# Loading the operands of an attention backward pass in nine pieces per pair of heads instead of seventeen

## The chip, the cores and the metric

The kernel runs on one core of a Trainium2 chip. A core has five engines with instruction streams of their own: TensorE (PE in the profile, PEld for its weight loads), VectorE (DVE), ScalarE (ACT), GpSimd (POOL) and SyncE (SP). They wait for one another through semaphores, and 16 DMA engines, shared by all queues, move data between HBM and the on-chip memory (SBUF). The metric is the device time of one execution in microseconds (us), lower is better; each time given is the median of several runs.

## What is computed

The reference is a transformer block (layer norm with modulation, softmax attention with 32 heads of 16 features over 2048 tokens and a width of 512, then a squared-ReLU MLP), its output, and the gradients of nine of its inputs. The change touches only the backward pass of the attention:

```python
scores = jnp.einsum('bhqd,bhkd->bhqk', q, k) * scale
p = _softmax(scores, axis=-1)
o = jnp.einsum('bhqk,bhkd->bhqd', p, v)
...
_out, _vjp = jax.vjp(_f, A_x, A_wqkv, A_wo, B_w1, B_b1, B_w2, B_b2, c, w_mod)
_grads = _vjp(grad_out)
```

For each head the backward pass forms the probabilities again (P = exp of Q K^T), the products dP = dO V^T, dS = P * dP, and from these the gradients dV = P^T dO, dK = dS^T Q and dQ = dS K.

## The kernel before

The program first runs the forward pass with much of the MLP in its shadow (`phase_fwd`, `phase5`'s setup), then `attn_bwd`, then the weight gradients and the input gradient (`phase6`). In `attn_bwd` the 32 heads are 8 groups of four (`g`), each handled as two pairs (`jp`). One such **pass** over a pair has 64 **steps**, one for each chunk `c` of 512 keys and each block `ib` of 128 queries. Four steps with the same `dsg` tile are called a **stretch** here (`m` from 0 to 15). The order of the instructions on each engine is as written: the scheduler is off in this phase.

A step does, for both heads `a` of the pair:

- PE computes the scores (`st`, line 1608), 64 rows of `QT` against `masked["KT"][a]`, in which only the rows of head `a` are not zero. ACT takes their exponential into `pu` (line 1611).
- PE computes dP of the step before (`dp`, line 1522), 64 rows of `dOT` against `masked["VT"][a]`. DVE multiplies it with `pu` into `ds` (line 1526); in some stretches, for one block, ACT copies it out and POOL multiplies instead (lines 1540 and 1541).
- PE accumulates dK and dV (`kv`, line 1459) some steps later, with the token-major `Q` and `dO` as weights.
- After four steps SP issues one DMA transpose of the 128 x 4096 tile `ds` into one of five buffers (`dsT`, line 1549; the fifth is part of `keep`). In one stretch of four PE transposes an eighth of it. Two such transposes feed eight `dq` calls (line 1484, weights from the token-major `K`); these are made in the even steps of the eight that follow the issue of the next two transposes' second one. So PE first needs a transposed tile about two stretches after the later of its two transposes was issued.

The operands lie in HBM in two forms. By features: `QTq_d`, `KTq_d`, `VTq_d`, `dOTq_d`, 128 rows for the four heads of a group, 32 rows for each, of 2048 tokens; a head uses rows 0 to 15 of its 32 for Q and K, and rows 0 to 17 for V and dO (two rows more, which carry the softmax's row term), and the other rows are zero. By tokens: `ktm_d` (128 x 2048 for a group), `qtm_d` and `dOp_d` (128 x 1024 each).

While group g is worked on, group g+1 is loaded into the other of two sets of tiles (names with a final g, and `q` or `keep` for the other set; the first two groups' loads fill whole tiles, all later ones only the rows that change). The list of these **pieces** is made by `load_group`; `pair_pieces` gives the four pieces of K^T and V^T for the next pair, and one or two pieces of a weight for the next phase (`wmt`) go between. The loop at lines 1594 to 1597 spreads a pass's pieces evenly over its 16 stretches. All are issued by POOL, in its instruction order, and before each stands a one-element copy from the `ds` tile of the stretch before (`tick`, line 1596), which holds POOL until DVE has begun that tile, so that the loads keep pace with the work. POOL's own multiplications (line 1541) stand in the same queue.

Of the kernel before, what the change touches and what calls it, by code (L numbers as in the profile page):

```python
# [19 lines left out]
P = 128  # L20
DH = 16
# [4 lines left out]
def chunks(total, size):  # L26
    out = []
    s = 0
    while s < total:
        w = min(size, total - s)  # L30
        out.append((s, w))
        s += w
    return out
# [72 lines left out]
class K:  # L106
# [1284 lines left out]
    def load_group(self, g):  # L1391

        S, ST, qp = self.S, self.ST, self.qp
        tm = {"K": self.ktm_d, "Q": self.qtm_d, "dO": self.dOp_d}
        fm = {"QT": (self.QTq_d, DH), "dOT": (self.dOTq_d, DH + 2)}
        width = {n: S if n in fm else ST * P if n == "K" else ST * 4 * DH for n in (*fm, *tm)}
        if g < 2:
            T, o = {}, 0
            for n, e in width.items():
                if g:  # L1400
                    T[n] = qp.tile([P, e], BF16, name=f"{n}g")[:]
                elif n == "K":
                    T[n] = self.keep[:, :e]
                else:
                    T[n] = self.q0[:, o:o + e]
                    o += e
            self.Tq[g] = T
        T, pieces = self.Tq[g % 2], []
        for n, (src, rows) in fm.items():
            if g < 2:  # L1410
                pieces += [(T[n][:, s0:s0 + sw], src[g, :, s0:s0 + sw]) for (s0, sw) in chunks(S, 1024)]
            else:
                pieces += [(T[n][r:r + rows, :], src[g, r:r + rows, :]) for r in range(0, P, 32)]
        for n, src in tm.items():
            pieces += [(T[n][:, a:a + 256], src[g, :, a:a + 256]) for a in range(0, width[n], 256)]
        return {n: t if n in fm else t.rearrange("p (st w) -> p st w", st=ST) for n, t in T.items()}, pieces

    def wq_pieces(self, t):
# [3 lines left out]

    def pair_pieces(self, g, jp):
        pieces = []
        for n, src, sh, rows in (("KT", self.KTq_d, 0, DH), ("VT", self.VTq_d, 2, DH + 2)):
            for j in (2 * jp, 2 * jp + 1):
                r = 32 * ((j + sh) % 4)
                pieces.append((self.masked[n][j % 2][r:r + rows, :], src[g, r:r + rows, :]))
        return pieces
# [536 lines left out]
```

## Time and profile before

| | |
|---|---|
| runs | 2509.63, 2515.87, 2516.81 us; median 2515.87 |
| profiled execution, first to last instruction (span) | 2498.5 us |
| median less this span | 17.4 us |
| attention backward | from 1166.9 us to about 2376.5 us of the span |
| busy in the whole span | PE 96%, ACT 91%, DVE 68%, POOL 30% |
| the 16 DMA engines | 90% busy or more in nearly every slice of the backward phase |

The profile does not give the profiled execution's time outside its span; if it was like the median of the runs, 17.4 us lie around the span. A page of the profile has, among others, the chain of work that ended last, the waits (which engine waited at which line for which other), groups of instructions with their mean duration, and the DMA queues: q1 is the hardware queue that carries SP's transposes, q0 the software queue that POOL issues to. For a line of DMA instructions, SPq and POOLq are the issuing sequencers, and "to landing" is the time from issue until the data is there.

### The profile page before, as it was taken

How to read it: one execution, taken by the hardware profiler on the slowest of the kernel's cores; microseconds unless marked ns; L12 is line 12 of the kernel's file. 1: busy time of each engine (PE TensorE's matmuls, PEld its weight loads, DVE VectorE, ACT ScalarE, POOL GpSimd, SP SyncE). 2: the span in 40 equal slices, each digit the busy share in tenths (PEclk: the TensorE clock that was granted, in tenths of full speed). 3: DMA queues.
4: the chain of work that ended last, by engine and by line, in shares of the span. 5: the costliest groups of instructions: out<-in, count | busy, mean ns of one | idle time of the engine just before them, and what ended most of it. 6: DMA issues, size and time to landing. Idle time of an engine off the chain costs nothing.

```text
span 2498.5 us, 67897 instructions
## 1 busy us (share of the span) xinstructions
PE 2410.2 (96%) x26211; PEld 1061.6 (42%) x26439; DVE 1695.0 (68%) x3487; ACT 2283.1 (91%) x3757; POOL 753.5 (30%) x1337
## 2 busy tenths in 40 slices
PE   8999999999999999999999999999999999999998
PEld 4555555555555555583233332333333333333343
DVE  6222322422332343576999999999999999999957
ACT  7999999999999997534999999999999999999945
POOL 2344531220131022245222323322333222322223
PEclk9999999999999999999999999999999999999999
DMA  4589661541243045499999999999999999999997
GB/s 166 135 179 208 169 125 47 132 100 40 92 114 98 23 123 147 110 199 216 232 235 233 232 227 231 237 234 231 230 235 239 234 230 236 234 233 236 238 217 192
DMA packets 1293547, 454.13 MB, mean 182 GB/s; under 512 B 1236948, under 2 KB 1261398, under 8 KB 1293222
## 3 DMA queue, kind: packets, MB, share of 16 engines
q1 hardware_dynamic: 1252422, 344.68, 71.8%
q0 software_dynamic: 38720, 104.04, 13.9%
q8 instruction: 207, 3.39, 0.6%
q10 hardware_dynamic: 2080, 1.05, 0.2%
q14 instruction: 118, 0.97, 0.1%
HBM read 75.83 MB, written 64.49 MB: 56 GB/s over the span
## 4 chain that ended last, share of the span: by engine, by line
PE 49%; ACT 35%; DMA 7%; issue 5%; DVE 3%; POOL 1%; SPq 1%; ACTq 0%; DVEq 0%; POOLq 0%
ACT pu L391 26%; PE st L1608 17%; PE acckv L1459 8%; ACT pu L1611 6%; DMA dsT<-ds 5%; PE accq L1484 5%; PE st L388 4%; PE dp L1522 2%; PE accbank L322 2%; PE dps L1050 2%; PE dp L1659 1%; PE st L1754 1%; ACT csq L1540 1%; PE pps L1237 1%; DVE ds L1526 1%
## 5 line engine op out<-in xcount | busy, mean ns | idle before, releaser
L1526 DVE TENSOR_TENSOR ds<-dp,pu 128x512 bf16<-128x512 f32 x1888 | 1166.0, 682 | 34.6 <-PE dp L1522 19.1
L1611 ACT ACTIVATE pu<-st 128x512 bf16<-128x512 f32 x2048 | 1073.8, 666 | 34.7 <-PE st L1608 21.3
L391 ACT ACTIVATE pu<-st 128x1024 bf16<-128x1024 f32 x992 | 912.1, 1077 | 4.2 <-PE st L388 3.7
L388 PE MATMUL st<-QTm,KTq 128*128 128x512 bf16 x1859 | 560.9, 377 | 27.1 <-ACT pu L391 6.1
L322 PEld LDWEIGHTS <-pu 128*128 128x128 bf16 x8192 | 346.7, 96 | 236.1 <-issue 3.0
L1522 PE MATMUL dp<-kvm,q 64*128 64x512 bf16 x1024 | 365.0, 384 | 2.0 <-DVE ds L1526 0.7
L322 PE MATMUL accbank<-Vaug,pu 128*128 128x17 bf16 x8192 | 357.4, 171 | 8.3 <-ACT Vaug L522 1.1
L1522 PE MATMUL dp<-kvm,dOTg 64*128 64x512 bf16 x1024 | 363.6, 383 | 0.3
L1608 PE MATMUL st<-kvm,q 64*128 64x512 bf16 x1024 | 349.4, 382 | 5.4 <-ACT pu L1611 0.2
L1608 PE MATMUL st<-kvm,QTg 64*128 64x512 bf16 x1024 | 348.1, 381 | 6.5
L1541 POOL TENSOR_TENSOR ds<-csq,pu 128x512 bf16<-128x512 f32 x128 | 147.2, 1150 | 627.0 <-ACT csq L1540 553.6
L388 PEld LDWEIGHTS <-KTq 128*128 128x128 bf16 x1984 | 188.4, 96 | 176.9 <-issue 124.8
L1459 PE MATMUL acckv<-ds,Qg 128*16 128x512 bf16 x1024 | 176.2, 382 | 0.3
L1459 PE MATMUL acckv<-pu,q 128*16 128x512 bf16 x1024 | 176.3, 383 | 0.0
L1459 PE MATMUL acckv<-ds,q 128*16 128x512 bf16 x1024 | 176.2, 383 | 0.0
L1459 PE MATMUL acckv<-pu,dOg 128*16 128x512 bf16 x1024 | 176.0, 382 | 0.0
L302 POOL DMA_DIRECT2D QTm<-QTq_d x124 | 63.1, 511 | 341.5 <-PE st L388 320.0
L1608 PEld LDWEIGHTS <-q 64*128 64x128 bf16 x1024 | 67.0, 94 | 163.5 <-issue 150.6
L1608 PEld LDWEIGHTS <-QTg 64*128 64x128 bf16 x1024 | 67.1, 94 | 160.6 <-issue 145.7
L329 DVE RECIPROCAL rl<-accbank 128x4 f32<-128x4 f32 x128 | 22.9, 179 | 158.3 <-PE accbank L322 158.2
L1522 PEld LDWEIGHTS <-q 64*128 64x128 bf16 x1024 | 88.8, 93 | 52.9 <-issue 43.3
L1522 PEld LDWEIGHTS <-dOTg 64*128 64x128 bf16 x1024 | 88.2, 93 | 52.9 <-issue 43.8
(390 smaller groups left out, 3055.1 us busy)
## 6 DMA issues: line engine op xcount, KB each, us to landing
KTq<-KTq_d POOLq DMA_DIRECT2D x24, 512.0 KB, 3.9
duT_d<-auT POOLq DMA_DIRECT2D x3, 1792.0 KB, 7.9
aT_d<-rT POOLq DMA_DIRECT2D x3, 1792.0 KB, 11.5
KTq_d<-KTq SPq DMA_DIRECT2D x32, 128.0 KB, 2.1
QTq_d<-ev_fm SPq DMA_DIRECT2D x32, 128.0 KB, 4.3
ktm_d<-ev_tm POOLq DMA_DIRECT2D x32, 128.0 KB, 2.5
VTq_d<-vT POOLq DMA_DIRECT2D x4, 1024.0 KB, 6.3
dx<-dx_d SPq DMA_DIRECT2D x16, 256.0 KB, 4.6
```

What stands on the lines that cost most here:

```text
L302: nc.gpsimd.dma_start(QTm[j][32 * j:32 * j + 32, :], self.QTq_d[g, 32 * j:32 * j + 32, 512 * qc:512 * (qc + 1)])
L322: nc.tensor.matmul(acc[:, a, sub, :], lhsT=pu[:, a, sub * P:(sub + 1) * P], rhs=Vaug[:, kb, h, :], start=(kb == 0 and a == 0 and sub == 0) ...
L388: nc.tensor.matmul(stt[:, a, :], lhsT=KT[:, kb * P:(kb + 1) * P], rhs=QTm[2 * jp + a][:], start=True, stop=True)
L391: nc.scalar.activation(pu[:], stt[:], ACT.Exp, scale=self.scale)
L1050: nc.tensor.matmul(pt[:], lhsT=a[st], rhs=g_tm[:, st, :], start=(st == 0), stop=(st == ST - 1))
L1459: nc.tensor.matmul(acckv[r:r + DH, :], lhsT=T[n][:, ib, col:col + DH], rhs=src[:, a, :], start=(ib == 0), stop=(ib == ST - 1))
L1484: nc.tensor.matmul(accq[r:r + 32, o:o + 256], lhsT=T["K"][:, 4 * c + sub, col:col + 32], rhs=v[:, r // 32 % 2 * 2:r // 32 % 2 * 2 + 2, 4 * ...
L1522: nc.tensor.matmul(dp[:], lhsT=T["dOT"][rd, ib * P:(ib + 1) * P], rhs=masked["VT"][a][rd, 512 * c:512 * (c + 1)], start=True, stop=True)
L1526: nc.vector.tensor_tensor(dsg[:, i, a], dp[:], pu[:, a, :], ALU.mult)
L1541: nc.gpsimd.tensor_tensor(dsg[:, i, 1], f[:], pu[:, 1, :], ALU.mult)
L1608: nc.tensor.matmul(stt[:], lhsT=T["QT"][rs, q], rhs=masked["KT"][a][rs, c0:c0 + 512], start=True, stop=True)
L1611: nc.scalar.activation(pu[:, a, :], stt[:], ACT.Exp, scale=self.scale)
```

## The change

For groups 2 to 7, Q^T comes in two pieces of 48 rows (two heads and the 16 rows between them) instead of four of 16, and dO^T in two of 64 rows instead of four of 18. By tokens, K, Q and dO come in pieces of 1024 columns instead of 256, for group 1 too: two, one and one instead of eight, four and four. V^T of each head comes as 32 rows instead of 18. The extra rows hold zeros or are multiplied by zeros, so the results are the same. The loads of group 0 stay as they were except for V^T's rows, and so do the weights' pieces and those of the last two passes.

```diff
         tm = {"K": self.ktm_d, "Q": self.qtm_d, "dO": self.dOp_d}
-        fm = {"QT": (self.QTq_d, DH), "dOT": (self.dOTq_d, DH + 2)}
+        fm = {"QT": (self.QTq_d, 32 + DH), "dOT": (self.dOTq_d, 64)}
...
-                pieces += [(T[n][r:r + rows, :], src[g, r:r + rows, :]) for r in range(0, P, 32)]
+                pieces += [(T[n][r:r + rows, :], src[g, r:r + rows, :]) for r in range(0, P, 64)]
         for n, src in tm.items():
-            pieces += [(T[n][:, a:a + 256], src[g, :, a:a + 256]) for a in range(0, width[n], 256)]
+            pieces += [(T[n][:, a:a + w], src[g, :, a:a + w]) for a, w in chunks(width[n], 1024 if g else 256)]
...
-        for n, src, sh, rows in (("KT", self.KTq_d, 0, DH), ("VT", self.VTq_d, 2, DH + 2)):
+        for n, src, sh, rows in (("KT", self.KTq_d, 0, DH), ("VT", self.VTq_d, 2, 32)):
```

Since a pass's pieces are spread evenly over its 16 stretches, fewer pieces also stand in other stretches. With 17 pieces there is about one in each; with nine they fall in stretches 0, 2, 4, 6, 8, 9, 11, 13 and 15. POOL has 1067 instructions in its list instead of 1283: 108 loads and 108 ticks fewer. The lists of PE, ACT and DVE are the same but for buffer numbers.

The first place is POOL's list in the first pass (group 0, first pair), where Q^T and dO^T of group 1 are loaded in four pieces of 128 rows x 1024 columns. `ds<-csq` and `ds<-junk_19880` are POOL's multiplications, `kvm` holds K^T and V^T, `QTg` and `dOTg` are the tiles of group 1. Before:

```order
 L1597 DMA WmT<-WmT_d 128x384
 L1541 TENSOR_TENSOR ds<-csq,pu 128x512
 L1596 COPY tick<-ds 1x1
 L1597 DMA QTg<-QTq_d 128x1024
 L1596 COPY tick<-ds 1x1
 L1597 DMA QTg<-QTq_d 128x1024
 L1541 TENSOR_TENSOR ds<-csq,pu 128x512
 L1596 COPY tick<-ds 1x1
 L1597 DMA dOTg<-dOTq_d 128x1024
 L1596 COPY tick<-ds 1x1
 L1597 DMA dOTg<-dOTq_d 128x1024
```

and now:

```order
 L1597 DMA WmT<-WmT_d 128x384
 L1596 COPY tick<-ds 1x1
 L1597 DMA QTg<-QTq_d 128x1024
 L1541 TENSOR_TENSOR ds<-csq,pu 128x512
 L1541 TENSOR_TENSOR ds<-junk_19880,pu 128x512
 L1596 COPY tick<-ds 1x1
 L1597 DMA QTg<-QTq_d 128x1024
 L1541 TENSOR_TENSOR ds<-csq,pu 128x512
 L1596 COPY tick<-ds 1x1
 L1597 DMA dOTg<-dOTq_d 128x1024
 L1541 TENSOR_TENSOR ds<-csq,pu 128x512
 L1541 TENSOR_TENSOR ds<-junk_19880,pu 128x512
```

The four loads stood in two couples, with one multiplication of POOL between the couples; now one or two multiplications stand between any two of them.

The second place is the end of a second pass and the start of the next, for the token-major Q and dO of group 2 (tile `q_19184`). Before, four loads of Q and four of dO of 256 columns stood there, of which this is the end:

```order
 L1597 DMA q_19184<-qtm_d 128x256
 L1596 COPY tick<-ds 1x1
 L1597 DMA q_19184<-dOp_d 128x256
 L1541 TENSOR_TENSOR ds<-csq,pu 128x512
 L1596 COPY tick<-ds 1x1
 L1597 DMA q_19184<-dOp_d 128x256
 L1541 TENSOR_TENSOR ds<-junk_19880,pu 128x512
 L1596 COPY tick<-ds 1x1
 L1597 DMA q_19184<-dOp_d 128x256
```

and now the two loads are:

```order
 L1597 DMA q_19184<-qtm_d 128x1024
 L1541 TENSOR_TENSOR ds<-csq,pu 128x512
 L1541 TENSOR_TENSOR ds<-junk_19880,pu 128x512
 L1596 COPY tick<-ds 1x1
 L1597 DMA q_19184<-dOp_d 128x1024
 L1541 TENSOR_TENSOR ds<-csq,pu 128x512
 L1596 COPY tick<-ds 1x1
 L1597 DMA kvm<-KTq_d 16x2048
```

The whole of dO now comes as the last load of the pass, behind POOL's two multiplications of stretches 13 and 14 and before the one of stretch 15.

## The prediction

> **What bounds the kernel now.** I first cut the backward phase into its 16 passes, at the first exponential of each, and read the busy times by window: the length of a pass, busy time and count of PE, of its weight loads, of DVE, ACT and POOL, the clock, the DMA share (over 1 where packets overlap) and GB/s.
>
> ```profile
> core 0: us, PE busy (x) PEld busy (x) DVE busy (x) ACT busy (x) POOL busy (x), PEclk, DMA share, GB/s
> 1166.90:1245.30 78.40, 72.92 (x704) 20.78 (x703) 73.06 (x119) 73.54 (x145) 22.30 (x40) 0.98 1.06 211
> 1245.30:1319.90 74.60, 73.91 (x805) 23.30 (x804) 73.36 (x119) 74.38 (x153) 21.48 (x41) 1.00 1.19 233
> ...
> 1470.30:1547.80 77.50, 74.82 (x805) 22.88 (x804) 73.61 (x119) 75.31 (x154) 22.60 (x45) 1.00 1.26 223
> ...
> 2148.90:2223.50 74.60, 73.92 (x805) 23.30 (x804) 73.34 (x119) 74.38 (x153) 22.78 (x45) 1.00 1.22 238
> 2223.50:2298.80 75.30, 74.36 (x805) 23.15 (x804) 73.57 (x119) 74.63 (x153) 18.08 (x31) 1.00 1.21 231
> 2298.80:2376.50 77.70, 75.03 (x817) 25.67 (x816) 74.04 (x121) 76.27 (x155) 22.29 (x43) 1.00 1.18 235
> sum 1209.60, PE 1187.48 PEld 371.20 DVE 1174.87 ACT 1194.52 POOL 356.14; mean PE 74.22 PEld 23.20 DVE 73.43 ACT 74.66 POOL 22.26
> ```
>
> A pass without a stall takes 74.6 us, and in it PE, ACT and DVE are all busy over 73 us. That is a floor which no load moves. What loads can move is the rest. The 14 passes from 1245.3 to 2298.8 take 1053.5 us, which is 14 x 74.6 = 1044.4 and 9.1 us more. The first pass has 78.4 - 74.6 = 3.8 us more, the last 3.1.
>
> The waits of the backward phase (from 1166 to 2390 us; total, times, longest) name what the rest is made of:
>
> ```profile
> POOL ds L1541 <- ACT csq L1540: 553.6, 115, 8.1
> ACT pu L1611 <- PE dp L1522: 9.3, 19, 2.8
> PE accq L1484 <- DMA dsT<-ds: 7.4, 12, 2.9
> PEld L1608 <- DMA keep<-ktm_d: 0.5, 2, 0.2
> ```
>
> POOL waits for the others and nobody waits long for it, so its instructions are free here. PE almost never waits for a loaded operand (0.5 us in two waits). It waits for late transposes, 12 times, and behind the waiting `accq` matmul stand the next scores and dP, so ACT and DVE lose the same time a little later. The instructions of line 1549 and their landing say how near the edge this is (ns min/median/max, then us):
>
> ```profile
> L1549 SPq DMA_TRANSPOSE dsT<-ds x208: 3490/4262/6457, 1173.4 to 2377.8; - x104
> ...
> DMA to landing us min/median/max: 5.1/7.2/9.0
> ```
>
> SP has one transpose to issue each 74.6/16 = 4.66 us, and issuing takes a median of 4.26. So SP and the DMA engines behind it have about 0.4 us to spare in each, some 6 us in a pass. A tile is wanted about two stretches, 9.3 us, after its issue was due.
>
> **What a load costs the transposes.** Of two passes, the quiet one from 2148.9 and the last from 2298.8, the DMA queue's packets, MB and share of 16 engines, and the last one's loads:
>
> ```profile
> q0 software_dynamic: 592, 1.16, 4.5%
> ...
> q0 software_dynamic: 768, 2.10, 7.8%
> ...
> keep<-xhat_d POOLq DMA_DIRECT2D x16, 128.0 KB, 4.1
> ```
>
> The quiet pass spends 4.5% of 74.6 us, 3.4 us of all 16 engines, on 1.16 MB: 2.9 us for 1 MB, 0.19 us for a piece of 64 KB and 0.76 for one of 256 KB. The bad case is in the first pass, where four pieces of 256 KB stand in two couples. POOL's rows, the queue from 1195 to 1215 us, the chain, and the wait in that pass:
>
> ```profile
> 1195.98 0.59 POOL L1597 DMA_DIRECT2D QTg<-QTq_d  x1
> ...
> 1197.78 0.54 POOL L1597 DMA_DIRECT2D QTg<-QTq_d  x1 [0.26 <-issue]
> ...
> 1204.86 0.58 POOL L1597 DMA_DIRECT2D dOTg<-dOTq_d  x1
> ...
> 1207.00 0.54 POOL L1597 DMA_DIRECT2D dOTg<-dOTq_d  x1 [0.26 <-issue]
> ...
> q0 software_dynamic: 304, 1.01, 20.9%
> ...
> 1206.13 11.04 DMA dsT<-ds
> ...
> PE accq L1484 <- DMA dsT<-ds: 2.9, 1, 2.9
> ```
>
> 20.9% of 20 us is 4.2 us for 1.01 MB, so 1.1 us for each 256 KB. A transpose issued among them landed after 11.04 us, PE waited 2.9 us for it, and the pass was 3.8 us over the floor. 11.04 - 2.9 = 8.1: a landing of up to about 8 us costs nothing, which is 0.9 us above the median.
>
> **The change, part by part.**
>
> *Fewer instructions on POOL.* 108 loads and 108 ticks go. Line 1597 by tile (ns min/median/max) and the tick's group in two passes from 1817 us (count, busy us, mean ns, idle before) give the price:
>
> ```profile
> L1597 POOL DMA_DIRECT2D Kg<-ktm_d x32: 534/565/580, 1214.5 to 2186.9; - x32
> L1597 POOL DMA_DIRECT2D kvm<-VTq_d x30: 498/544/568, 1179.2 to 2245.3; - x30
> ...
> L1596 POOL COPY tick<-ds 1x1 bf16<-1x1 bf16 x34 | 6.0, 176 | 13.8 <-DVE ds L1526 13.8
> ```
>
> About 0.56 + 0.18 us each, 80 us in all, whatever a load's size, but of an engine that is busy 22 us of a pass and issues for 17 x 0.56 = 9.5 more, out of 75. Worth nothing in time; if POOL were the bound it would be worth the 80.
>
> *More bytes.* A group's loads were 2304 KB: 256 for K^T, 288 for V^T, 192 of weights, 256 for Q^T, 288 for dO^T, 512, 256 and 256 by tokens. Now V^T and dO^T are 512 each and Q^T is 384, in all 2880 KB, a quarter more. At 2.9 us for 1 MB the 0.29 MB more of a pass take 0.85 us of DMA time, at the first pass's price 1.2. Either fits in the 6 us to spare, so in the sum it costs 0; without that room it would cost 14 x 0.85 = 12 us.
>
> *The first pass.* Its couples are taken apart: as the rows of order show, one or two of POOL's multiplications stand between any two of the four loads, which fall in stretches 9, 11, 13 and 15, about 9 us apart. One piece then costs a transpose about 1 us, from a median of 7.2 to 8.2 us, at the edge. I take back 3 of the 3.8 us; the ends are 3.8 and 0.
>
> *The other 14 passes.* In the first half of a pass there is now one piece of 64 to 128 KB in two stretches where there were two of 64 to 72, so what is late there gets a little better. In the second half four pieces of 192 to 256 KB stand about 9 us apart, each instead of two of 64 to 72. A transpose that meets one is later by 0.76 to 1.1 us, where before it met two at 0.2 each: 0.4 to 0.7 us worse. The waits start at about 8 us, above the median of 7.2, so a part of the transposes crosses it. I put the gain and the loss at about 3 us each and take 0. The ends are -9.1 us (every stall gone) and +53 (each pass stalls as the first did, 14 x 3.8).
>
> *Operands that land later as one piece.* The whole of dO now comes last, in stretch 15, while dK and dV of the next group first want it in that group's fourth step. In POOL's order it stands right behind the multiplication of stretch 14, so it is issued a stretch and more before the pass ends, 8 us before its use. The rows of 256 KB before:
>
> ```profile
> QTg<-QTq_d POOLq DMA_DIRECT2D x2, 256.0 KB, 5.1
> dOTg<-dOTq_d POOLq DMA_DIRECT2D x2, 256.0 KB, 7.6
> ```
>
> 5.1 to 7.6 us, the latter in the bunch; that hides it. Landing 1 us beyond would cost 1 us in each of 6 changes of group.
>
> Sum: 0 + 0 - 3 + 0 + 0 = -3 us. The profiled span of 2498.5 us becomes 2495.5, and with the 17.4 us by which the median of the runs is longer, **2513 us**.
>
> A rule that speaks against the change: the Trainium skill, "DMA: Bandwidth & Descriptors", section "Queues, rings and completion order", says that each DMA engine takes turns between its queues a packet at a time and drains a packet before it switches. By it a piece four times as large makes the transposes' small packets take turns with four times as many large ones, and the loads win time from the transposes out of proportion; the first pass's 11.04 us agrees with that.
>
> **The rivals.**
>
> *All stalls go.* If the late transposes come from loads that POOL issues close together, nine pieces with POOL's multiplications between them end both kinds, and 3.8 + 9.1 = 12.9 us go: 2503. For it speaks the first pass, where a bunch was the cause; against it that the quiet passes carry as many loads as the others. The Trainium skill's "DMA: Bandwidth & Descriptors", section "Rules for kernel authors", is on this side: it would have many small transfers made into one large. No run here shows that yet.
>
> *The large pieces delay the transposes: slower.* Place: stretches 9 to 15, where a pass now loads 0.9 to 1 MB in less than half its time. The last pass has that density throughout (2.10 MB) and is 3.1 us over the floor. Seven of 16 stretches of it, 1.4 us, in 14 passes is 19 us, less 3 of the first: 2516 + 16 = 2532. It decides as soon as the transposes that meet a large piece land after more than 8 us in most passes. For it: the same mechanism as in the first pass. Against it: the last pass also issues `dq` twice as fast, which may be its excess, and its loads of 128 KB land in 4.1 us.
>
> *Nothing moves.* The first pass's stall has another cause (it is the start of the phase, its clock is 0.98), and all else is hidden: 2516.
>
> **Chances and range.** The forecast 0.5, with its own range 2508 to 2520; all stalls go 0.2; slower 0.2; nothing moves 0.1. About 0.3% (7.5 us, 2508.3 to 2523.4) is what a measurement of this kernel can tell from no change. Faster by more than that is the second case and a tenth of the first, 0.25; slower most of the third and a little of the first, 0.19; the rest, 0.56, is the same. For 8 in 10 the range takes in half of the cases at both ends: 2503 to 2528.
>
> **What would show it.** In the changed profile the first pass should fall from 78.4 to about 75.4 us with no transposes landing after 9 us; the 14 passes should still sum to 1053.5 us within some 6; PE's wait for `dsT` should be 5 to 8 us; POOL's line 1597 should have 108 fewer instructions, and its busy time in a pass should fall by the eight ticks, 1.4 us. SP's transposes should keep a median near 4.3 us. The forecast is wrong if the passes are quiet at 74.6 throughout, or if `accq` waits for `dsT` in most passes at stretches 10 to 15, or if PE's weight loads wait for `dO` or `K` at a change of group.

## The result and the profile after

| | before | changed |
|---|---|---|
| median of the runs, us | 2509.48 (6 runs, 2506.85 to 2516.81) | 2528.25 (6 runs, 2518.51 to 2537.72) |
| ratio, with its 95% interval | 1 | 1.0074 (1.0048 to 1.0100) |
| profiled execution: span, us | 2498.5 | 2535.5 |

The change makes the kernel 0.7% slower, about 19 us. The profiled execution of the change took 2537.72 us, 2.2 more than its span, and is the longest of its six runs; the one of before, whose span is shorter than any of its six runs by 8 us or more, was at the quick end. So the spans are 37 us apart and the medians 19: read the profiles for places, the medians for sizes.

The backward phase of the changed kernel by pass, cut as before (columns as in the prediction's first fence):

```profile
core 0: us, PE busy (x) PEld busy (x) DVE busy (x) ACT busy (x) POOL busy (x), PEclk, DMA share, GB/s
1167.30:1242.90 75.60, 71.96 (x704) 20.86 (x703) 72.83 (x119) 73.31 (x146) 18.26 (x28) 1.00 1.04 214
1242.90:1321.00 78.10, 75.83 (x806) 22.86 (x804) 73.47 (x119) 74.95 (x154) 17.40 (x29) 0.98 1.18 231
1321.00:1405.00 84.00, 77.39 (x805) 22.86 (x804) 73.63 (x119) 75.39 (x154) 17.36 (x29) 0.94 1.21 213
...
1712.00:1787.10 75.10, 74.36 (x806) 23.39 (x804) 73.50 (x120) 74.53 (x154) 17.43 (x29) 1.00 1.21 240
...
1941.10:2023.30 82.20, 76.73 (x806) 22.97 (x805) 73.55 (x120) 75.34 (x153) 17.31 (x29) 0.96 1.20 222
...
2174.60:2255.50 80.90, 75.92 (x805) 22.97 (x804) 73.36 (x119) 75.08 (x154) 17.38 (x29) 0.96 1.16 224
2255.50:2330.40 74.90, 74.31 (x807) 23.14 (x805) 73.31 (x120) 74.54 (x154) 18.08 (x31) 1.00 1.17 234
```

The first pass fell from 78.4 to 75.6 us. The 14 passes after it (1242.9 to 2330.4) take 1087.5 us where they took 1053.5, and very unevenly: 75 to 78 us in most, 81 to 84 in three. A pass of 84 us holds nearly the same DVE and ACT work as one of 75, so the rest is waiting. The clock column reads 0.94 to 0.96 in the three long passes, in which PE is idle for 5.0 to 6.6 us, and 1.00 in the two of 75 us, in which it is idle for 0.6 and 0.7. The waits of that phase (1166 to 2408 us) say for what:

```profile
DVE ds L1526 <- PE dp L1522: 47.5, 59, 5.4
ACT pu L1611 <- PE dp L1522: 36.2, 31, 4.8
PE accq L1484 <- DMA dsT<-ds: 17.6, 15, 4.4
PE accq L1484 <- DMA keep<-ds: 10.8, 4, 4.2
```

PE waited 28.4 us for transposed tiles (`dsT` and `keep`), where it had been 7.4; nearly all of it is in stretches 10 to 15. DVE and ACT wait behind PE. No weight load waits over 0.2 us for an operand. The transposes' own line:

```profile
L1549 SPq DMA_TRANSPOSE dsT<-ds x208: 3489/4288/8943, 1173.9 to 2409.3; - x104
L1549 SPq DMA_TRANSPOSE keep<-ds x48: 3486/4302/8098, 1192.6 to 2332.1; - x48
...
DMA to landing us min/median/max: 5.1/7.4/12.4
```

The medians hardly moved (4.26 to 4.29 us to issue, 7.2 to 7.4 to land); the worst issue went from 6.5 to 8.9 us, and 8 of the 256 now take SP more than 6 us, where there were 2. The worst landings in these lines are 9.0 and 12.4 us, but the traces give a landing for only 64 of the 256 transposes before and for 96 now; the 11.04 us of the first pass before is not among them. A few transposes are held up for long. One of them is in the pass from 1941.1. POOL's rows (start, duration), SP's, and two windows:

```profile
2000.84 0.18 POOL L1596 COPY tick<-ds 1x1 bf16<-1x1 bf16 x1 [1.56 <-DVE ds L1526]
2001.30 0.56 POOL L1597 DMA_DIRECT2D q<-dOTq_d  x1 [0.29 <-issue]
```

```profile
2000.55 4.34 SPq L1549 DMA_TRANSPOSE dsT<-ds  x1
2004.98 8.86 SPq L1549 DMA_TRANSPOSE dsT<-ds  x1
```

```profile
1998.00:2005.00 7.00, 6.95 (x82) 2.34 (x80) 7.00 (x13) 7.00 (x16) 1.89 (x3) 1.00 1.07 240
2005.00:2012.00 7.00, 3.48 (x34) 1.01 (x31) 4.26 (x7) 4.40 (x9) 1.15 (x1) 0.91 1.39 102
```

The load of dO^T for stretch 13 is issued at 2001.30, 0.75 us after SP began to issue a transpose. It lands 9.8 us later. From 2005 to 2012 all 16 DMA engines are busy (share 1.39) and move 102 GB/s instead of 240; the next transpose takes SP 8.86 us, and PE works 3.5 of 7 us.

### The profile page after: what moved, and what is told of

Same layout as the page of the kernel before. It is cut to its first block, busy times and chain, and to the rows that moved or that the text cites. A ratio compares the mean times of both kernels' runs of the same rounds, so it can differ in the third digit from the quotient of the medians.

```text
span 2535.5 us, 67723 instructions
## 1 busy us (share of the span) xinstructions
PE 2439.4 (96%) x26439; PEld 1061.5 (42%) x26439; DVE 1693.8 (67%) x3487; ACT 2286.5 (90%) x3757; POOL 681.7 (27%) x1121
## 3 DMA queue, kind: packets, MB, share of 16 engines
q0 software_dynamic: 37184, 107.92, 14.9%
## 4 chain that ended last, share of the span: by engine, by line
PE 55%; ACT 24%; DMA 12%; issue 4%; DVE 3%; POOL 1%; SPq 0%; ACTq 0%; DVEq 0%; POOLq 0%
ACT pu L391 18%; PE st L1608 16%; PE st L388 8%; PE acckv L1459 8%; DMA dsT<-ds 8%; ACT pu L1611 5%; PE accq L1484 5%; PE accbank L322 3%; DMA keep<-ds 2%; PE dp L1522 2%; PE dps L1050 2%; PE pps L1237 2%; PE dp L1659 1%; PE pps L631 1%; PE st L1754 1%
## 5 line engine op out<-in xcount | busy, mean ns | idle before, releaser
L388 PE MATMUL st<-QTm,KTq 128*128 128x512 bf16 x1984 | 587.5, 377 | 20.5 <-ACT pu L391 6.1
L1608 PEld LDWEIGHTS <-q 64*128 64x128 bf16 x1024 | 67.0, 94 | 165.0 <-issue 151.9
L1484 PE MATMUL accq<-dsT,Kg 128*32 128x256 bf16 x1696 | 103.6, 282 | 15.3 <-DMA dsT<-ds 15.2
L1484 PE MATMUL accq<-dsT,keep 128*32 128x256 bf16 x1632 | 106.7, 279 | 7.3 <-DMA dsT<-ds 7.1
```

The source lines that it names most:

```text
L388: nc.tensor.matmul(stt[:, a, :], lhsT=KT[:, kb * P:(kb + 1) * P], rhs=QTm[2 * jp + a][:], start=True, stop=True)
L1484: nc.tensor.matmul(accq[r:r + 32, o:o + 256], lhsT=T["K"][:, 4 * c + sub, col:col + 32], rhs=v[:, r // 32 % 2 * 2:r // 32 % 2 * 2 + 2, 4 * ...
L1608: nc.tensor.matmul(stt[:], lhsT=T["QT"][rs, q], rhs=masked["KT"][a][rs, c0:c0 + 512], start=True, stop=True)
```

## The experiments

Ratios are to runs of the kernel before on the same chip in the same hour. Its median was between 2505.2 and 2513.5 us from hour to hour, so runs of different groups compare to about 0.3%, not better.

The edits are shortened: what a line has besides the part that changes is left out, and so is the old rule, which stays for passes that do not have nine loads.

**Is it the loads, and is it their size as one DMA?** Two runs: the kernel before without the operands' loads in passes 3 to 14 (only the weights' pieces stay there), and the changed one with each large piece issued as four DMAs one behind the other, at the same nine places.

```diff
 # e_noload (on the kernel before)
-  pieces = self.pair_pieces(g, 1) + wmt[2 * g:2 * g + 1] + later[:cut]
+  pieces = (self.pair_pieces(g, 1) + wmt[2 * g:2 * g + 1] + later[:cut]) if g < 1 or Tn is None else wmt[2 * g:2 * g + 1]
...
-  pieces = self.pair_pieces(g + 1, 0) + later
+  pieces = self.pair_pieces(g + 1, 0) + later if g < 1 else wmt[2 * g + 1:2 * g + 2]
 # e_cut4 (on the change), for pieces of 1024 columns and for those of 48 or 64 rows
-  nc.gpsimd.dma_start(*pieces.pop(0))
+  for s0 in range(0, w, w // 4):
+      nc.gpsimd.dma_start(dst[:, s0:s0 + w // 4], src[:, s0:s0 + w // 4])
```

> The kernel before without any load of attention operands for groups 2 to 7 (their K, Q, dO, Q^T, dO^T, K^T and V^T are left out, so the gradients of A_x and A_wqkv are not the reference's; the weights' pieces and the last pass's loads stay). Theory (all that the changed kernel lost is transposes that meet loads): the passes without loads take 74.6 us each, PE waits under 1 us in all for dsT in them, and the kernel is 7 to 10 us faster than before (about 2501). Rival (transposes are late by themselves, since SP issues one after another without a pause): these passes still show PE waiting for dsT and average 75 us or more, and the time is within 3 us of before.

> The changed kernel with each large piece cut again into four DMAs of 48 to 64 KB, issued one behind the other at the same place. Theory (the bytes that stand at one place, and the moment, decide; not the number of DMAs): like the changed kernel, 2520 to 2535, PE waiting 20 us or more for dsT, at the same stretches. Rival (one DMA of 256 KB holds the DMA engines in a way that four of 64 KB do not): like the kernel before, within 5 us of 2510.

Without loads: 2497.69 us, ratio 0.9956 (0.9937 to 0.9974), 9 us faster as expected; its passes without loads take 74.6 to 74.9 us. The first pass, which keeps its loads and its bunch, took 82.0 in this profile. So the floor was read rightly. With four DMAs: 2548.98 us, ratio 1.0155 (1.0114 to 1.0196), a miss: slower than expected, and slower than the change itself. One large DMA is not the trouble in itself; what it brings at its place and time is.

**The tick, and other places.** In the change the tick of a load waits for the first block of the stretch before. Here it waits for the third block; in the second run the loads also stand at other, odd stretches.

```diff
 # e_tick
-  nc.gpsimd.tensor_copy(tick[:], last[7][0:1, 0, 0, 0:1])
+  nc.gpsimd.tensor_copy(tick[:], last[7][0:1, 2, 1, 0:1])
 # e_odd: the same, and the nine pieces at
+  m >= (1, 1, 3, 5, 7, 9, 11, 13, 15)[9 - len(pieces)]
```

> The changed kernel, but the tick before each load reads the last element that DVE has written of the stretch before (block 2, head 1) instead of its first, so that the pieces of stretches 9 and 13 are issued some 3.5 us later and no longer a stretch early. Theory (a large piece costs time only if it meets the transpose of an odd stretch, whose tile PE wants first; the pieces of 9 and 13 meet those of 7 and 11): the long stretches 10 and 14 go back to 4.5 us, PE's wait for dsT falls from 33 to under 12 us and the kernel to 2505 to 2515. Rival (the size alone decides, whichever transpose is met): PE's wait stays over 20 us, 2520 to 2535.

> The kernel of e_tick with the nine pieces of passes 0 to 13 in stretches 1, 1, 3, 5, 7, 9, 11, 13, 15, so that the small ones too are issued at the start of an odd stretch and meet the transpose of an even one. Theory (which transpose is met decides): no worse than e_tick and under the kernel before, 2500 to 2508, with PE waiting under 6 us for dsT. Rival (size alone decides): as the changed kernel, 2520 to 2535.

With the later tick: 2508.01 us, ratio 1.0002 (0.9985 to 1.0019). The same nine loads with the same bytes lose nothing against before, once the early ones come about 3 us later. The transposes' line of that run:

```profile
L1549 SPq DMA_TRANSPOSE dsT<-ds x208: 3415/4254/6368, 1173.7 to 2384.1; - x104
...
  PE accq L1484: 12.3, 12
DMA to landing us min/median/max: 5.0/7.3/10.0
```

At odd stretches: 2513.56 us, 1.0022 (1.0006 to 1.0038), a miss: this schedule put two loads of K^T in stretch 1, and the longest wait of PE for a tile in its first 15 passes (2.3 us) is in stretch 2 of the second pass, with another of 1.3 us in stretch 2 of the third.

**Which of the loads.** In a pass of the change the large loads stand at stretches 9, 11, 13 and 15. The delay is given to two of them.

```diff
-  nc.gpsimd.tensor_copy(tick[:], last[7][0:1, 0, 0, 0:1])
+  nc.gpsimd.tensor_copy(tick[:], last[7][0:1, 2, 1, 0:1] if m in (9, 13) else last[7][0:1, 0, 0, 0:1])
 # e_late1115: (11, 15) instead of (9, 13)
```

> The changed kernel, with one edit: the tick ahead of the loads of stretches 9 and 13 waits for the third block of the stretch before instead of its first; the loads of stretches 11 and 15, as large, keep their tick. Theory (the loss is the meeting of those two loads with the transposes of stretches 7 and 11, whose tiles the matmuls want soonest): nearly all of the loss goes, 2506 to 2516 us against 2528, ratio to the kernel before 1.000 to 1.004, and TensorE waits under 15 us in accq for dsT and keep tiles. Rival (any large load costs the transposes the same, and delaying all four simply spreads them better): half of the loss goes, 2517 to 2523 us.

> The changed kernel, with the mirror edit: only the tick ahead of the loads of stretches 11 and 15 is delayed by two blocks. Theory (the loads of 9 and 13 do the harm): next to nothing changes, 2522 to 2532 us, and TensorE still waits over 25 us in accq for dsT and keep. Rival (all four loads share the loss): half of it goes, 2517 to 2523 us.

Loads of 9 and 13 delayed: 2506.74 us, ratio 0.9995 (0.9980 to 1.0010). Loads of 11 and 15 delayed: 2529.40 us, ratio 1.0093 (1.0059 to 1.0127). The waits of PE for the tiles of line 1549 (us, times), the first run first:

```profile
  PE accq L1484: 10.4, 12
```

```profile
  PE accq L1484: 24.9, 25
```

The whole loss against the kernel before hangs on when two loads of nine are sent, and these are no larger than the two others. What sets them apart stands in the code: POOL multiplies in the odd stretches and in 10 and 14. A load for stretch 11 or 15 waits behind the multiplication of the stretch before; stretches 8 and 12 have none, so the loads for 9 and 13 follow their tick at once.

**The parts of the change.** Each on the kernel before, word for word as in the change's diff: only K, Q and dO by tokens (11 loads in a pass), only Q^T and dO^T (15 loads), only V^T's rows.

> The kernel before with one part of the change: only K, Q and dO by tokens in pieces of 1024 columns. Twelve pieces per pair's second half, so 11 loads in a pass, and the four large ones stand last in the odd passes, at stretches 11, 12, 14 and 15; the even passes keep small loads only. Theory (a large load costs where it meets the transpose of stretch 7 or 11 and nothing elsewhere): between nothing and a third of the loss, 2508 to 2520 us, longer passes among the odd ones only. Rival (the cost goes by the number of large loads, 28 of the 56 of the change): half of the loss, 2517 to 2523 us.

> The kernel before with the other part: only Q and dO by features in two loads each (48 and 64 rows). It leaves 15 loads in a pass, and from the third pair on the four large ones stand at stretches 6, 7, 8 and 9 of the even passes, one after another, with 64 KB loads behind them. Theory (bytes that meet a transpose in a short time): the bunch makes the transposes late as the four 256 KB loads do in the first pass of the kernel before, which loses 3.8 us there; six even passes at 2 to 5 us each, so 2520 to 2540 us, and the stalls sit at stretches 9 to 11 of the even passes. Rival (only stretches 9 and 13 are bad places): a quarter of the loss or less, 2509 to 2515 us.

> The kernel before with one part of the change: only the V^T rows, 32 instead of 18 in each of their four loads per pass (128 KB instead of 72 KB). Theory (a load of this size among 17 evenly spread ones costs the transposes about 1 us more each, which the slack of the stretches takes): no change, 2503 to 2512 us. Rival (the forecast's price per byte without slack, 4 x 0.19 us in 16 passes): 12 us slower, about 2520 us.

By tokens alone: 2501.09 us, ratio 0.9973 (0.9958 to 0.9988), faster than before, where a time between no change and a third of the loss was expected. By features alone: 2527.99 us, ratio 1.0081 (1.0058 to 1.0103), as slow as the whole. V^T's rows: 2508.76 us, ratio 0.9995 (0.9978 to 1.0013). In the second of these the large loads follow one another in stretches 6 to 9, and its stalls sit mostly at stretches 8 and 10 of the even passes (counted from 0), about where the expectation put them. That loads which come close together are a second way to lose, apart from the one above, fits this; it is not shown, since no run has this part with the later tick.

**Putting the good parts together.** The loads by tokens with the later tick at two stretches or everywhere; and small loads throughout, with the second group's Q^T and dO^T in 64 KB pieces as well.

```diff
 # e_tm913, e_tmtick: the change's line for tm, and the tick of e_late913 or of e_tick
 # e_small (on the kernel before): the tick of e_tick, and
-  for (s0, sw) in chunks(S, 1024)]
+  for (s0, sw) in chunks(S, 256 if g else 1024)]
```

> Merged K, Q and dO by tokens as in the part alone (2501.1 us), and the tick ahead of the loads of stretches 9 and 13 two blocks later. Those stretches hold 256 KB loads in the first two passes only, so the theory says: the first pass falls from 78.7 to 74.3 to 75.5 us as in the changed kernel with that tick (74.3), the rest stands; 3 to 4 us faster than the part alone, 2496 to 2500 us, ratio to the kernel before 0.995 to 0.997. Rival (the first pass loses to the bunch of its loads, not to their place): as the part alone, 2500 to 2503 us.

> The same merged loads by tokens, with the tick of every load two blocks later. Theory: as with the tick of stretches 9 and 13 alone, since the loads of the other places cost nothing where they stand: 2496 to 2501 us. Rival (a later tick brings loads of other stretches into the transposes that matter, as the odd stretches' schedule of the changed kernel did): 2503 us or more.

> The kernel before with its small loads throughout: also the second group's Q and dO by features, four 256 KB loads in the first pass, are cut in 64 KB ones (256 columns), and the tick of every load is two blocks later. Theory (the first pass loses 3.8 us to that bunch): the first pass falls from 78.4 to about 75 us, the others stand; 2502 to 2506 us. Rival (bytes in a time count, and 16 small loads bring as many): the first pass stays over 77 us, 2506 to 2512 us.

2500.15 us, ratio 0.9982 (0.9960 to 1.0004); 2497.67 us, ratio 0.9966 (0.9951 to 0.9981); 2500.23 us, ratio 0.9974 (0.9960 to 0.9988). All three first passes take 74.2 us. The first run is a miss in time: 1 us faster than the part by tokens alone, where 3 to 4 were expected. The later tick everywhere does no harm, and in the third run the gain was larger than expected.

**Place or bunch.** Two explanations of the loads of 9 and 13 were left: the place (they meet the transposes of stretches 7 and 11, and of two tiles that `dq` reads together the odd stretch's is the later one), or a bunch (the load of 13, sent early, is one stretch behind the load of 11). One run puts every large load on an odd stretch's transpose, far from its neighbours, with the later tick; the other leaves the early ones early and takes their neighbours away.

```diff
 # e_even: the tick of e_tick, and
+  m >= (0, 1, 3, 5, 6, 8, 10, 12, 14)[9 - len(pieces)]
 # e_apart: the change's own tick, and
+  m >= (0, 1, 2, 3, 4, 6, 9, 13, 15)[9 - len(pieces)]
```

> The changed kernel with every tick two blocks later and the large loads at stretches 8, 10, 12 and 14 instead of 9, 11, 13 and 15 (the five smaller ones at 0, 1, 3, 5 and 6): just as evenly spread, two stretches apart, but each meets the transpose of an odd stretch (7, 9, 11, 13), whose tile is the later of the two that the matmuls read together. Place theory: the loss of the change is back or larger, 2520 to 2535 us, TensorE waits over 25 us in accq for dsT and keep. Bunch theory (two loads within a stretch do the harm): none of it, 2503 to 2513 us, and under 15 us of that wait.

> The changed kernel with its own early tick, the loads at stretches 0, 1, 2, 3, 4, 6, 9, 13 and 15: the large ones of 9 and 13 are still released a stretch early and meet the transposes of 7 and 11, but the load of WmT that went ahead of the first stands at 4, and the large load that went ahead of the second (11) stands at 6. Place theory: the loss stays, 2518 to 2530 us, with transposes of stretches 7 and 11 landing in over 8 us at the median. Bunch theory: it goes, 2503 to 2513 us, and the transposes of 7 and 11 land in under 7.8 us at the median.

2506.17 us, ratio 0.9971 (0.9949 to 0.9993), and 2546.72 us, ratio 1.0137 (1.0112 to 1.0162). Both explanations fall: large loads on odd stretches' transposes cost nothing, and the early loads without their neighbours cost more than in the change. By the count below, 26 large loads come within 0.95 us after the start of a transpose's issue in this run, against 13 in the change, where the load of 9 often stands behind a smaller one of stretch 8 and comes a little later; seven smaller loads do so too. Of the second run:

```profile
L1549 SPq DMA_TRANSPOSE dsT<-ds x208: 3451/4386/7488, 1172.2 to 2420.8; - x104
...
  PE accq L1484: 41.1, 34
```

What the harmful loads share is when they come within a transpose's issue. The same dO^T load of the same pass in the first of these runs, with POOL's rows, SP's transposes on either side, and two windows:

```profile
1990.37 0.18 POOL L1596 COPY tick<-ds 1x1 bf16<-1x1 bf16 x1
1990.49 0.57 POOL L1597 DMA_DIRECT2D q<-dOTq_d  x1
```

```profile
1986.63 4.67 SPq L1549 DMA_TRANSPOSE dsT<-ds  x1
1991.40 4.64 SPq L1549 DMA_TRANSPOSE dsT<-ds  x1
```

```profile
1986.00:1991.00 5.00, 4.80 (x50) 1.55 (x46) 4.98 (x8) 5.00 (x11) 1.73 (x3) 1.00 1.34 203
1991.00:1998.00 7.00, 7.00 (x79) 1.88 (x76) 6.61 (x12) 7.00 (x15) 1.21 (x2) 1.00 1.26 279
```

It is issued 3.9 us after one transpose and 0.9 us before the next. The DMA engines keep moving 279 GB/s, and PE is busy for all of the 7 us. The landing of these loads in the two runs, the change first, then the harmless one (KB each, median us):

```profile
dOTg<-dOTq_d POOLq DMA_DIRECT2D x8, 256.0 KB, 5.7
q<-dOTq_d POOLq DMA_DIRECT2D x6, 256.0 KB, 5.9
```

```profile
dOTg<-dOTq_d POOLq DMA_DIRECT2D x8, 256.0 KB, 4.6
q<-dOTq_d POOLq DMA_DIRECT2D x6, 256.0 KB, 4.8
```

**The phase alone.** The large loads stand in the stretches of the two harmless runs (e_even and e_tick), but every tick waits for the last block of the stretch before, and the loop stands behind the step that issues that block's transpose.

```diff
+  if i == 0:
+      while pieces and m >= (0, 1, 3, 5, 6, 8, 10, 12, 14)[9 - len(pieces)]:      # e_ph_odd
+          nc.gpsimd.tensor_copy(tick[:], last[7][0:1, 3, 1, 0:1])
+          nc.gpsimd.dma_start(*pieces.pop(0))
 # e_ph_even: (0, 1, 3, 5, 7, 9, 11, 13, 15)
```

> The changed kernel with the large loads at stretches 8, 10, 12 and 14 as in the harmless run (2506 us), but every tick waits for the last block of the stretch before, and stands in the program behind the step that issues that stretch's transpose: the loads should come 0.5 to 1.5 us after the issue of the transposes of stretches 7, 9, 11 and 13 instead of 0.6 us ahead of it. Phase theory: these transposes land late, 9 us or more at the median, and the loss is back, 2525 to 2560 us, ratio over 1.006. Rival (the harm lies in stretches 8 and 12 themselves, say in what else runs there, and not in the phase): 2503 to 2515 us.

> The same late tick with the large loads at stretches 9, 11, 13 and 15: they come as long after the issue of a transpose, but of stretches 8, 10, 12 and 14. Phase and odd stretch together decide: those transposes land late, but their tiles are read only with the next one's, a stretch of 4.7 us later, and the time stays at 2503 to 2515 us. Phase alone decides: 2525 to 2560 us as its twin.

2562.62 us, ratio 1.0253 (1.0201 to 1.0306), and 2586.14 us, ratio 1.0332 (1.0284 to 1.0380). By the ratios, about a microsecond's shift costs 2.8% and 3.3% against the harmless runs, some 70 and 80 us, both more than expected, though only half of the loads come in the harmful phase (the count below). Odd or even stretch makes no rescue: the loss on even ones is even larger, so the phase needs no help from the place. PE's waits in the run on odd ones:

```profile
DVE ds L1526 <- PE dp L1522: 65.7, 82, 3.7
ACT pu L1607 <- PE dp L1522: 53.0, 55, 3.4
PE accq L1484 <- DMA dsT<-ds: 32.7, 30, 2.6
...
PE accq L1484 <- DMA keep<-ds: 11.0, 10, 3.0
```

**The phase without the merging.** The kernel before with its 17 small loads, with the harmful tick and with the later one.

```diff
 # e_b_ph: the loop and tick of e_ph_odd, with the old spreading of 17 pieces
 # e_b_tick: the one line of e_tick
```

> The kernel before with its 17 small loads, the tick on the last block of the stretch before, standing behind the step that issues that stretch's transpose, as in the two runs that lost 57 and 81 us. Theory (the phase opens the loss, the KB in it set its size): the loads carry on average half as much as the nine, and two often follow one another, so between a quarter and two thirds of that loss, 2520 to 2550 us. Rival (the phase alone, whatever the size): 2555 us or more. Rival (only loads of 128 KB and more can hold a transpose up): under 2515 us.

> The kernel before with the tick of every load two blocks later, so that the 17 small loads come ahead of a transpose's issue or well after it begins. Theory (some of the kernel's 9 us above its floor is this phase too): 2498 to 2504 us, with the first pass still above 76 us or, if its bunch suffered from the phase, at 74 to 75. Rival (its small loads cost nothing in any phase): as before, 2504 to 2510 us.

2550.61 us, ratio 1.0146 (1.0118 to 1.0174), and **2494.09 us, ratio 0.9931 (0.9909 to 0.9953)**. The first lies at the upper edge of what was expected, the second beyond the gain that was. The second is the fastest of all, beats both kernels, and differs from the kernel before in one line. Its transposes, and its first two and its last pass:

```profile
L1549 SPq DMA_TRANSPOSE dsT<-ds x208: 3524/4228/7562, 1174.3 to 2370.5; - x104
...
  PE accq L1484: 4.5, 4
DMA to landing us min/median/max: 5.2/6.9/8.6
```

```profile
1167.80:1242.90 75.10, 71.70 (x704) 20.87 (x703) 72.89 (x119) 73.14 (x145) 22.59 (x40) 1.00 1.07 221
1242.90:1317.60 74.70, 74.10 (x805) 23.30 (x804) 73.47 (x119) 74.48 (x153) 21.80 (x41) 1.00 1.16 229
...
2291.70:2368.90 77.20, 74.73 (x816) 25.68 (x816) 74.04 (x120) 76.19 (x155) 22.70 (x43) 1.00 1.18 237
```

**A count over the runs.** From the issue times of POOL's loads and SP's transposes in each profile, the loads of the passes that come 0 to 0.95 us after SP began to issue a transpose, and their MB (of 1024 KB):

| run | such loads, of all | MB in them | us |
|---|---|---|---|
| e_tick / e_even | 0 / 0 of 147 | 0 / 0 | 2508.0 / 2506.2 |
| e_late913 | 2 of 147 | 0.2 | 2506.7 |
| e_odd | 6 of 148 | 0.4 | 2513.6 |
| e_late1115 | 12 of 147 | 2.7 | 2529.4 |
| the change | 14 of 147 | 3.2 | 2528.3 |
| e_cut4 | 73 of 315 | 4.5 | 2549.0 |
| e_apart | 33 of 147 | 6.7 | 2546.7 |
| e_ph_odd / e_ph_even | 72 / 69 of 147 | 10.2 / 10.0 | 2562.6 / 2586.1 |
| e_b_tick | 1 of 255 | 0.1 | 2494.1 |
| the kernel before | 22 of 255 | 1.6 | 2509.5 |
| e_v32 | 28 of 255 | 2.1 | 2508.8 |
| e_b_ph | 134 of 255 | 9.5 | 2550.6 |
| e_fm | 11 of 231 | 1.1 | 2528.0 |

Within the kernels with nine places for loads and within those with 17 loads the time rises with those MB, by some 5 to 10 us for each where there is more than 1 MB: (2528.3 - 2508.0) / 3.2 = 6.3 and (2550.6 - 2494.1) / 9.4 = 6.0. The part by features (e_fm) is off this line by some 25 us. The limit of 0.95 us was chosen with the results in hand, and the kernel before depends on it: up to 1.25 us, 82 of its loads count, with 5.9 MB, and 34 of the change's, with 7.3 MB.

## Why the prediction was wrong

The forecast was 2513 us and no change; the measured 2528.25 us lies 15 us above it and just beyond the range, which ended at 2528. Against the kernel before the forecast was -3 us, and the measurement is +19. The second of the three rivals, slower at 2532 us, was the case that came.

- **The floor** (74.6 us a pass; loads can only move what lies above) held: 74.6 to 74.9 us in the second to fourteenth pass of the run without loads.
- **The first pass** (-3 us) came out in the profile: 78.4 to 75.6. One profile doesn't price it, though: with its nine loads in the same places that pass took 75.6, 77.3 (e_late1115) and 78.7 us (e_tm, V^T's smaller rows), and the first pass of before took 78.4 and, unchanged in e_noload, 82.0. In the eight runs whose tick waits for the third block, at all loads or at those of 9 and 13, it took 74.2 to 75.8 us.
- **The other 14 passes** (a gain and a loss of 3 us each, taken as 0) is the step that failed. In the profile they rose by 34 us, PE's wait for tiles from 7.4 to 28.4. I let each large load delay a transpose by a fixed 0.76 to 1.1 us, on a median landing that rests on the 64 transposes whose landing the trace gives. The runs show no fixed price: with the loads of stretches 9 and 13 sent about 3 us later and nothing else changed, the loss is gone (0.9995), so what a load of 256 KB costs depends on when it is issued within a transpose's issue. What PE waits for is a few very late transposes (one of 12.4 us), and a median can't show them. I had listed the places of the loads and held the spreading for an improvement; the tick and POOL's multiplications, which set the time within a stretch, stood in the rows of order that I quoted, and I didn't follow them to SP's issues.
- **The slower rival** had the right sign, the right stretches (its sign to look for, `accq` waiting at stretches 10 to 15, is what happened) and nearly the right size, but a wrong cause: "that density" of 0.9 to 1 MB in half a pass. The run with the later tick has the same density and 2508 us. A bunch may be what costs the part by features (1.0081); that isn't shown.
- **Fewer instructions on POOL** at 0: nothing contradicts it. POOL's busy time in a pass fell from about 22.6 to 17.4 us, not by the 1.4 that I named, since a pass has eight loads fewer as well as eight ticks. **Operands that land later** at 0: right, 0.2 us.
- **More bytes** at 0, with 0.85 us of DMA time in a pass: the queue's share of the span rose from 13.9% to 14.9%, (0.149 x 2535.5 - 0.139 x 2498.5) = 31 us of all 16 engines, or 2 us in a pass and not 0.85. In the backward phase the queue's packets took 3.2 us of all 16 engines for 1 MB before and 3.8 in the change, so not only the bytes grew. V^T's part alone, 224 of the 576 KB that a group loads more, cost nothing.
- **The 17.4 us around the span** were wrong as well: the profiled execution of the change has 2.2, and the later runs of before have 1.8. The runs of before had only been slower than its profile.

How the loss of 0.7% divides stays open. The early tick costs both kernels: taking it away brings the change from 1.0074 to 1.0002 and the kernel before to 0.9931, 0.7% each. With the later tick in both, the nine loads are still 0.7% behind the 17 (1.0002 and 0.9931); other pairs with hardly a load in the harmful phase give 0.4% (e_even, 0.9971) and nothing (e_even and e_small, 0.9971 and 0.9974), with about 0.3% of uncertainty in each. By the count, the change has 1.6 MB more in the harmful phase, some 10 of the 19 us at 6 us for a MB, if the limit of 0.95 us is right. So the runs show that the phase of two loads is where the changed kernel loses its 0.7%, and that a later tick wins it back; they don't show that the phase alone is why it is slower than the kernel before. Between none and about all of the 19 us may lie in the larger loads outside that phase. The parts point to the loads by features: those by tokens are the faster for being merged.

On merging, the Trainium skill's "DMA: Bandwidth & Descriptors", section "Rules for kernel authors", has many small transfers made into one large. Here the part by tokens agrees (64 to 256 KB, ratio 0.9973), the part by features doesn't (1.0081), and the best of all is the kernel with the small ones (0.9931).

## What to carry to other kernels

Where a stream of DMAs is nearly saturated and an engine lives on its deadline, ask of each other transfer not only how large it is and how many stand near, but when it starts within the stream's own rhythm, and look for the few transfers that are held up and the waits behind them, not at the median. The wait that releases a load is a tuning knob of its own: one index in it was worth 0.7%, and wrong by a microsecond cost 2 to 3%. When a schedule is thinned out, check which loads lose the instruction that had held them back.

## What the runs showed of the hardware

How late a POOL load begins goes with SP's issue. Over the 448 loads of over 150 KB in eight of the runs (e_tick, e_even, e_late913, e_late1115, the change, e_apart, e_ph_odd, e_ph_even), by the time of their issue relative to the start of a transpose's issue (first packet and landing in us after the load's issue, medians; the first packet only of loads that no other POOL load in flight hides, their number in brackets; transposed data in the 10 us from the issue, KB in a us):

| issue, us | loads | first packet | landing | transposed |
|---|---|---|---|---|
| -0.9 to -0.5 | 168 | 1.5 (166) | 3.9 | 206 |
| 0 to 0.3 | 22 | 1.4 (22) | 4.5 | 190 |
| 0.3 to 0.6 | 36 | 3.6 (36) | 7.3 | 169 |
| 0.6 to 0.9 | 34 | 4.8 (29) | 8.1 | 178 |
| 0.9 to 1.3 | 30 | 4.9 (8) | 7.0 | 206 |
| 2 to 3 | 32 | 2.9 (32) | 4.9 | 201 |

Except in the second row, the first packet moves at the median 0.0 to 1.4 us after SP has done issuing the transpose that is under way (4.2 to 4.4 us), whenever the load was issued. So a load that comes 0.3 to 1.3 us behind a start waits longest, and up to 0.9 us the transposes lose about a sixth of their rate; one that comes just ahead of a start does neither. In the second row the load begins at once, and SP's own issue takes 6.1 us at the median. At 0.9 to 1.3 us the load is late too, partly because in 22 of the 30 cases another load was still in flight, but the transposes' rate no longer suffers. Why isn't settled. The ticks all wait on DVE, so a load's place in DVE's rhythm moved together with its place in SP's, and no run takes the two apart. The Trainium skill's "DMA: Bandwidth & Descriptors", section "SWDGE vs HWDGE vs iDMA", says that POOL's and SP's transfers feed different queues inside each DMA engine, which takes turns between them; by that alone one would expect a load to start after the same time in any phase, and here it starts after 1.4 to 4.9 us. The same section says that VectorE in one of its modes locks POOL out of the memory in which POOL writes its descriptors, which no run here could show.
